# The first attention group in plain 128-key blocks, with the probabilities as matmul weights and copies on the chip for the second group

## The chip, the cores and the metric

The kernel runs on 1 core of one Trainium2 chip. Its time is the device time of one launch in microseconds (us), as the median of the runs that are fast. Engines are named as in the profile: PE is TensorE, PEld its weight loads, DVE is VectorE, ACT is ScalarE, POOL is GpSimd, SP is SyncE. A number like L728 is a line of the kernel that was profiled, so the same piece of code has another number in another version.

## The reference, cut to what matters

```python
# attention: batch 4, heads 8, sequence 768, head_dim 64; n_sink 4, window 64
# is_retrieval = [1, 0, 1, 0, 0, 0, 1, 0]
scores = (q @ k.T) / sqrt(64)
causal = rel >= 0                                  # rel = query position - key position
stream_keep = causal & (is_sink | (rel < window))  # heads 1, 3, 4, 5, 7
mask = causal for heads 0, 2, 6 else stream_keep
a = exp(scores masked - max); a = a / (a.sum(-1) + 1e-9)
x = (a @ v) reshaped to [3072, 512]
# mixture of 4 experts over all 3072 rows
p = domain_probs / (domain_probs.sum(-1) + 1e-9)
out = sum over e of p[:, e] * (relu(x @ w1[e]) @ w2[e])    # w1 512x1024, w2 1024x512
```

## The kernel before: the parts that the change touches

The 3072 rows are worked in eight groups of 384 queries (4 batches, two chunks each). A group is its attention, then four experts. PE runs group g's experts with the attention of group g+1 woven in between. Only the first group's attention has nothing to lie beside, so everything that it takes is in the time of the kernel. That stage, and the hand-over to group 1, is what the change rewrites.

In the kernel before, the first group uses the same forms as the others. Streaming heads take tiles of 96 keys with the four sink keys put in front of each; those sink rows are copied on DVE:

```python
def sink_row(b, h, c):                       # [cut: L261 is this copy]
    t = v_tile(b, c, h)[:, :, own(h)]
    nc.vector.tensor_copy(
        out=t[0:NS, TC * c : TC * (c + 1), :],
        in_=t[R0 : R0 + NS, 0:1, :].to_broadcast([NS, TC, D]),
    )
...
for h in range(H):                           # q and k of the first group: 16 loads
    nc.sync.dma_start(out=k32[:, :, h, :], in_=rows_of(k, 0, h, 0))
    nc.scalar.dma_start(out=q32[:, :, h, :], in_=rows_of(q, 0, h, 0))
nc.scalar.add_instruction(...)               # load of the table of functions, behind them
...
# values(h), cut: v is the weight, the probabilities move; 64 more columns of ones
# give the sum, and the quotient is exp(-ln(sum)) on ACT
nc.tensor.matmul(out=ps[:, q0 : q0 + nq], lhsT=v_tile(b, c, h)[:, t, :],
                 rhs=es[:, o : o + nq], ...)
nc.scalar.activation(out=rc[r, :], in_=ps[o, 0:CH], func=AF.Ln, bias=eps[o, :])
nc.scalar.activation(out=rc, in_=rc, func=AF.Exp, scale=-1.0)
nc.vector.tensor_tensor(out=xT[g][r, hp, :], in0=ps[r, 0:CH], in1=rc[r, :], op=ALU.mult)
...
def bank():                                  # scores, transposes and experts share these
    return pA.tile([P, 512], FP32, name="pA", bufs=4)
...
warm_up(ps_warm, 8, 512)
for _ in attention(0, 0):
    pass
zero(gp, kRr)                                # POOL memsets, behind POOL's weight loads
zero(gp, kSr)
mask_w()
# [cut] loop over groups: attention(g + 1) is woven into moe_group(g)
begin = {0: 0.2, 1: 1.0}.get(g, 0.0) * UNIT  # where the weaving begins
```

The softmax here doesn't subtract the row's maximum and nothing guards it: scores larger than these inputs give would overflow.

## Time and profile before

| what | value | read from |
|---|---|---|
| time | 414.77 us, 3 runs (413.07 to 414.81) | the runs |
| span of the profiled run | 413.1 us | head of the page |
| PE busy | 395.8 us (96%) | busy table of the page |
| granted PE clock | 1.00 in every stretch of the first 60 us | windows |
| first exponent on ACT | 9.09 us | timeline |
| first expert matmul, first relu | 24.30 us, 26.93 us | timeline |
| PE waits beside group 1's first transposes | 0.29 and 0.95 us | timeline |

The runs of this kernel fall on two values, about 413.07 and 414.8 us, so its median moves between these from one set of rounds to the next; a difference under 1.5 us says little unless the rounds are many. PE is busy from 24 us to the end. The stage up to the first relu is therefore the one place where time can be saved, and waits on PE beside group 1 are the one place where a change to this stage can add some. PSUM is the memory that PE's matmuls write to; a bank is a part of it. A warm-up is a matmul on a dummy tile, whose result nobody reads. Two timeline columns are read throughout: the start of a group of instructions (first number) and, in brackets at the end, how long its engine was idle just before and what ended that.

### The profile page before, as it was taken

Reading aid. Unit: us, or ns where it says so; the run is one execution under the profiler, and the core shown is the slowest. Engines: PE = TensorE matmul, PEld = TensorE weight load, DVE = VectorE, ACT = ScalarE, POOL = GpSimd, SP = SyncE. Lnnn points to the kernel's source line nnn. Section 1 sums busy time; section 2 is a strip of 40 time slices with the busy share of each in tenths; the row PEclk is TensorE's granted clock in tenths of the full one; section 3 lists DMA queues with packets and bytes.
Section 4 is the critical chain, followed back from the end, with each engine's and each line's share of the span. In section 5 each row is a group of like instructions: output and inputs, shape, how many; then the busy total and the mean of one; then the engine's idle time right before and its main releaser. Section 6 shows DMA issues by size and latency. Waiting matters only on the chain.

```text
span 413.1 us, 6801 instructions
## 1 busy us (share of the span) xinstructions
PE 395.8 (96%) x2670; PEld 222.4 (54%) x2670; DVE 155.8 (38%) x302; ACT 240.9 (58%) x509; POOL 141.7 (34%) x176
## 2 busy tenths in 40 slices
PE   6799999999999999999999999999999999999996
PEld 3565555555555555555555555555555555555552
DVE  7975553223433325233333333233343222432222
ACT  2676874336876547656665448566565477653331
POOL 8938618359359177002930085000000000000000
PEclk9999999999999999999999999999999999999999
DMA  9999999999989999058984999259002000020002
GB/s 173 142 195 204 209 208 133 136 210 124 174 64 181 217 75 101 27 107 147 111 53 96 182 72 77 17 108 166 2 2 76 5 2 0 2 76 2 1 2 76
DMA packets 159988, 40.83 MB, mean 99 GB/s; under 512 B 150364, under 2 KB 154836, under 8 KB 159956
## 3 DMA queue, kind: packets, MB, share of 16 engines
q0 software_dynamic: 102592, 20.98, 59.5%
q1 hardware_dynamic: 54164, 18.62, 21.7%
q10 hardware_dynamic: 3200, 0.79, 0.9%
q8 instruction: 21, 0.34, 0.3%
q14 instruction: 11, 0.09, 0.1%
HBM read 43.57 MB, written 6.29 MB: 121 GB/s over the span
## 4 chain that ended last, share of the span: by engine, by line
PE 86%; ACT 6%; DVE 4%; DMA 2%; issue 1%; ACTq 0%; DVEq 0%
PE pO L749 40%; PE pA L728 36%; PE pV L609 5%; PE pA L561 4%; ACT hs L741 2%; DMA q<-in_q_dram 2%; ACT rc L628 2%; DVE kS L490 1%; ACT rc L638 1%; DVE vS L261 1%; ACT es L579 1%; DVE kR L474 1%; DVE qT L465 0%; PE pO L355 0%; PE pV L355 0%
## 5 line engine op out<-in xcount | busy, mean ns | idle before, releaser
L728 PE MATMUL pA<-xT,w1sb 128*128 128x384 f16 x1024 | 187.4, 326 | 3.9 <-ACT hs L741 2.5
L749 PE MATMUL pO<-w2sb,hs 128*128 128x512 f16 x768 | 180.8, 379 | 0.0
L741 ACT ACTIVATE hs<-pA 128x384 f16<-128x384 f32 x256 | 122.1, 494 | 95.9 <-PE pA L728 89.1
L728 PEld LDWEIGHTS <-w1sb 128*128 128x128 f16 x1024 | 96.8, 98 | 65.5 <-issue 5.5
L749 PEld LDWEIGHTS <-hs 128*128 128x128 f16 x768 | 72.7, 98 | 74.3 <-ACT hs L741 0.6
L765 DVE SCALAR_TENSOR_TENSOR acc<-pO,p_sb,acc 128x512 f32<-128x512 f32 x72 | 53.9, 749 | 99.5 <-PE pO L749 98.9
L579 ACT ACTIVATE es<-pA 128x512 f16<-128x512 f32 (+3 forms) x122 | 61.0, 511 | 22.7 <-PE pA L561 20.9
L628 ACT ACTIVATE rc<-pV,eps 64x384 f32<-64x384 f32 x60 | 34.5, 575 | 33.0 <-PE pV L609 32.0
L204 POOL DMA_DIRECT2D kSr<-in_k_dram x30 | 30.1, 1006 | 36.5 <-issue 14.7
L250 POOL DMA_DIRECT2D vS<-in_v_dram x30 | 30.4, 1024 | 34.8 <-PE pV L609 34.0
L633 DVE TENSOR_TENSOR xT<-pV,rc 64x384 f16<-64x384 f32 x60 | 33.1, 552 | 4.2 <-PE pA L728 1.7
L583 DVE TENSOR_TENSOR es<-es,mW 128x384 f16<-128x384 f16 x30 | 10.8, 360 | 57.2 <-ACT es L579 57.2
L638 ACT ACTIVATE rc<-rc 64x384 f32<-64x384 f32 x58 | 30.2, 521 | 1.8
L761 DVE TENSOR_SCALAR acc<-pO,p_sb 128x512 f32<-128x512 f32 x24 | 18.0, 749 | 34.3 <-PE pO L749 33.0
L200 POOL DMA_DIRECT2D kRr<-in_k_dram x18 | 14.1, 783 | 47.2 <-DMA kR<-kRr 43.2
L583 DVE TENSOR_TENSOR es<-es,mC 128x256 f16<-128x256 f16 (+1 forms) x42 | 10.8, 257 | 45.4 <-ACT es L579 45.0
L561 PE MATMUL pA<-qT,kR 128*128 128x384 f16 (+2 forms) x120 | 25.0, 278 | 0.4
L609 PE MATMUL pV<-es,vR 128*128 128x384 f16 (+2 forms) x120 | 21.6, 278 | 0.0
L246 POOL DMA_DIRECT2D vR<-in_v_dram x24 | 19.2, 800 | 4.3 <-DMA w2sb<-in_moe_w_dram 4.2
L561 PEld LDWEIGHTS <-kS 128*128 128x128 f16 x255 | 13.9, 98 | 9.5 <-issue 2.9
L561 PE MATMUL pA<-qT,kS 128*128 128x55 f16 (+4 forms) x255 | 16.6, 195 | 2.2 <-ACT es L579 1.6
L609 PEld LDWEIGHTS <-vS 128*128 128x128 f16 x255 | 13.2, 98 | 9.1 <-DVE vS L261 3.0
(77 smaller groups left out, 161.3 us busy)
## 6 DMA issues: line engine op xcount, KB each, us to landing
out_dram<-acc SPq DMA_DIRECT2D x24, 256.0 KB
w1sb<-in_moe_w_dram POOLq DMA_DIRECT2D x4, 1024.0 KB, 14.5
w2sb<-in_moe_w_dram POOLq DMA_DIRECT2D x4, 1024.0 KB, 17.5
kSr<-in_k_dram POOLq DMA_DIRECT2D x30, 112.0 KB, 3.8
vS<-in_v_dram POOLq DMA_DIRECT2D x30, 112.0 KB, 3.8
q<-in_q_dram POOLq DMA_DIRECT2D x18, 128.0 KB, 4.4
vR<-in_v_dram POOLq DMA_DIRECT2D x24, 48.0 KB, 4.1
kRr<-in_k_dram POOLq DMA_DIRECT2D x18, 48.0 KB, 4.1
```

The lines of the kernel that those rows point to most:

```text
L204: gp.dma_start(out=kSr[:, :, SH.index(h), own(h)], in_=windows_of(k, b, h, c),)
L250: gp.dma_start(out=t[:, :, own(h)], in_=windows_of(v, b, h, c))
L561: nc.tensor.matmul(out=ps[:, o : o + nq], lhsT=key_tile(b, c, h, t), rhs=qTs[b, c][:, hp, q0 : q0 + nq], start=(n == 0 or not first), stop ...
L579: nc.scalar.activation(out=es[:, 0:cols], in_=ps[:, 0:cols], func=AF.Exp, scale=SC)
L609: nc.tensor.matmul(out=ps[:, q0 : q0 + nq], lhsT=v_tile(b, c, h)[:, t, :], rhs=es[:, o : o + nq], start=(n == 0), stop=(n == len(work) - 1 ...
L628: nc.scalar.activation(out=rc[r, :], in_=ps[o, 0:CH], func=AF.Ln, bias=eps[o, :])
L633: nc.vector.tensor_tensor(out=xT[g][r, hp, :], in0=ps[r, 0:CH], in1=rc[r, :], op=ALU.mult)
L638: nc.scalar.activation(out=rc[r, :], in_=rc[r, :], func=AF.Exp, scale=-1.0)
L728: nc.tensor.matmul(out=pss[ft][:, 0:CH], lhsT=w1sb[:, e * DMP + ct, ft * P : (ft + 1) * P], rhs=xT[g][:, ct, :], start=(ct == 0), stop=(ct ...
L741: nc.scalar.activation(out=hs[:, ft, :], in_=ps[:, 0:CH], func=AF.Relu)
L749: nc.tensor.matmul(out=ps_o, lhsT=hs[:, ft, j * P : (j + 1) * P], rhs=w2sb[:, e * FTP + ft, :], start=(ft == 0), stop=(ft == FTP - 1),)
L765: nc.vector.scalar_tensor_tensor(out=acc[nt], in0=ps_o, scalar=p_ap, in1=acc[nt], op0=ALU.mult, op1=ALU.add,)
```

## The change

The intent is a shorter first stage. Keys come in plain blocks of 128, with a band of biases for the streaming heads, so no sink rows are needed in that stage. In the value matmuls the probabilities are the weights, and v with one column of ones moves: 12 matmuls of 65 columns for a pair of heads. The quotient is then per row, done by DVE, and PE transposes the result. Half the heads of q and k, and all of v, come through GpSimd loads whose pieces are three rows long; PE puts v's rows in order again with a selection matrix. Since the next group expects keys and values in the old tiles, 37 small DVE copies make these afterwards.

```diff
-    for h in range(H):
-        nc.sync.dma_start(out=k32[:, :, h, :], in_=rows_of(k, 0, h, 0))
-        nc.scalar.dma_start(out=q32[:, :, h, :], in_=rows_of(q, 0, h, 0))
+    HF = H // 2
+    for h in range(HF):
+        nc.sync.dma_start(out=qk32[:, 1, :, h, :], in_=rows_of(k, 0, h, 0))
+        nc.scalar.dma_start(out=qk32[:, 0, :, h, :], in_=rows_of(q, 0, h, 0))
...
+    load_triples(v, v16, 0, 0)
+    band()
+    load_triples(k, qk16[:, 1, :, :, :], 0, 0, HF)
+    load_triples(q, qk16[:, 0, :, :, :], 0, 0, HF)
+    band_with_sinks()
...
+        def scores_own(h):                       # 64 rows, 64 rows, then biases: 128 rows
+            ps = bank()
+            score(ps, 0, h, 2, P, True)
+            score(ps, P, h, 0, CH, False)
+            if RETR[h]:
+                add(ps, 0, bC)
+            else:
+                add(ps, 0, bW[:, 0:P])
+                add(ps, P, bWs)
+            own_of[h] = exp(ps, 512)
...
+        def v_blocks():                          # 9 matmuls of 512 columns, 3 casts
+            for t in range(3):
+                ps = pO.tile([P, DM], FP32, name="pO", bufs=2)
+                for j in range(3):
+                    x = t * P - j + 2
+                    nc.tensor.matmul(out=ps, lhsT=pick[:, x : x + P], rhs=v16[:, :, j, :],
+                                     start=(j == 0), stop=(j == 2))
+                nc.vector.tensor_copy(out=v0[t][:, :, 0:D], in_=...)
...
+        WARM = [4, 4, 6, 8, 2, 2, 4, 4]          # warm-ups before values and quotients
+        transposes(0); scores_own(0); transposes(1); scores_own(1)
+        scores_shared(0, 2); scores_shared(1, 3)
+        transposes(2); v_blocks(); values(0); scores_own(2); scores_own(3)
+        transposes(3); values(1); to_xT(0, ...)
+        # [cut] the same for the other two pairs
...
+    def keep_for_next():
+        copy = nc.vector.tensor_copy
+        for h in range(H):                       # 4 copies a retrieval head, 5 a streaming one
+            ...
-    for _ in attention(0, 0):
-        pass
+    first_attention()
+    small_things()
+    keep_for_next()
```

(The calls that stand on one line here with semicolons stand on lines of their own in the kernel.)

## The prediction

> **What bounds the kernel now.** I read the busy table by stage first, then the chain of waits, then the timelines of the first 33 us. The view of windows (columns: stretch, its length, then busy us of PE, PEld, DVE, ACT and POOL with instruction counts, clock, DMA share, GB/s) gives, joined from two questions:
>
> ```profile
> 12.00:14.00 2.00, 1.31 (x9) 0.87 (x9) 1.94 (x6) 1.41 (x4) 2.00 (x3) 1.00 1.19 70
> 14.00:16.00 2.00, 1.47 (x16) 1.17 (x17) 1.93 (x7) 0.99 (x2) 2.00 (x4) 1.00 0.96 135
> 16.00:18.00 2.00, 0.87 (x7) 0.53 (x6) 2.00 (x1) 1.95 (x6) 2.00 (x3) 1.00 1.11 205
> ...
> 24.50:62.00 37.50, 34.64 (x267) 20.06 (x266) 22.46 (x43) 27.50 (x62) 18.09 (x25) 1.00 1.28 205
> 62.00:100.00 38.00, 37.73 (x215) 20.14 (x213) 9.54 (x16) 18.28 (x39) 26.26 (x29) 1.00 1.70 152
> ```
>
> From 62 us on PE has nothing left to gain; from 24.5 to 62 it idles 37.50 - 34.64 = 2.9 us. The change edits nothing after the first group but the work put in front of group 1. So it can pay only by letting the first expert matmuls start earlier, and cost only by making PE wait beside group 1. The timeline shows how the first stage runs and ends (start, us, engine, line, operation, count, idle before):
>
> ```profile
> 7.80 1.28 ACT L330 ACT_TABLE_LOAD   x1 [7.80 <-DMA q<-in_q_dram]
> 9.09 0.87 ACT L579 ACTIVATE es<-pA 128x512 f16<-128x512 f32 x2
> ...
> 12.83 1.63 DVE L261 COPY vS<-vS 4x256 f16<-4x256 f16 x1
> 15.73 2.72 DVE L261 COPY vS<-vS 4x256 f16<-4x256 f16 x1
> 21.30 0.22 DVE L261 COPY vS<-vS 4x256 f16<-4x256 f16 x1
> ...
> 24.30 3.09 PE L728 MATMUL pA<-xT,w1sb 128*128 128x384 f16 x16
> 25.96 0.56 DVE L633 TENSOR_TENSOR xT<-pO,rc 64x384 f16<-64x384 f32 x1 [0.60 <-ACT rc L638]
> 26.93 1.64 ACT L741 ACTIVATE hs<-pA 128x384 f16<-128x384 f32 x4 [1.01 <-PE pA L728]
> ```
>
> The scores' exponent starts only at 9.09, because ACT issues eight q loads (the later four wait for earlier ones) before its table load. Two tiny copies of sink values hold DVE 1.6 and 2.7 us and PE behind them. The first relu, the real end of the stage, is at 26.93. Then group 1's transposes need DVE at once:
>
> ```profile
> 27.94 0.79 DVE L474 CAST kR<-pA 64x384 f16<-64x384 f32 x1 [1.43 <-PE pA L457]
> 28.77 0.81 DVE L490 CAST kS<-pA 64x384 f16<-64x384 f32 x1
> 29.63 0.36 PE L457 MATMUL pA<-ident,q 128*64 128x128 f16 x6 [0.29 <-DVE kS L490]
> 31.91 0.82 PE L728 MATMUL pA<-xT,w1sb 128*128 128x384 f16 x4 [0.95 <-DVE kS L490]
> ```
>
> Here the reader sees that PE's expert matmuls and the transposes share four PSUM banks, so that PE already stops (0.29, 0.95 us) until DVE has emptied one.
>
> **What the Trainium skill says.** (1) "SBUF — State Buffer", section "Who interferes with whom": a DVE copy in a two-port mode and a GpSimd instruction take one shared port pair as an exclusive lock. The trace agrees: the same 4x256 copy takes 0.22 us at 21.30 and 2.72 us at 15.73, while POOL runs memsets back to back. (2) "VectorE: DVE Perf Modes", section "The TRN2 errata": 58 + FD/4 cycles at 0.96 GHz for a 16-bit SBUF copy, that is 0.08 us at 64 elements; for 128x256 it gives 0.127, and the trace has 0.14 from the mask copy at 21.55 to the next at 21.69. (3) Same page, section "Two Vector instructions with no wait between them": an instruction that starts in another 32-partition quadrant is held until the one before has finished. The trace fits: after the 0.54 us cast to partitions 0 to 63 at 5.60, the one to 64 to 127 starts at 6.17; the next, in the same quadrant, follows after 0.48. (4) "TensorE: Matmul & The Clock Gate", Part 1: about 3.4 us of idle PE halve its clock. PE's longest wait in this trace is 1.7 us (at 7.28), so no run shows it yet.
>
> **The change part by part.**
>
> *Loads and start.* HWDGE loads fall from 16 to 8; ACT's fourth issue ends at 2.97 in the trace, so the table load ends near 4.3, not 9.09. PE's eight cold warm-up matmuls still run until 4.65, so the first transposes stay at 4.65. The first exponent: K transposes end 4.99, K cast ready 5.76; q copy on ACT ready 6.03; score and mask 0.33 plus 0.21 latency (traced between a matmul's last column and its reader): 6.6 instead of 9.1, 2.5 us early.
>
> *Until the values.* Then transposes(1), its ACT copy, and own scores of head 1 at 8.04; two shared tiles to 9.14. Transposes(2) needs the half loaded by GpSimd: POOL order from traced durations (masks 1.5, issues 0.8 to 0.9 each, selects 0.56) puts the issue of k at 5.3 and q at 6.1; with 3.6 us landing I estimate 9.8 for q. The row-ordering of v is new PE work: 9 matmuls of 512 columns at 0.216 = 1.94 us, the third block held for one of two pO banks. Its last cast, 0.70 us, is ready at 13.37. So the first values finish at 13.95; before, heads 0 and 1 had theirs at 15.0. The 2.5 us have shrunk to about one.
>
> *PE in order from 13.6.* Issue slots: 128 columns 0.056, 384 columns 0.1625; a value matmul with 65 columns 0.06 (traced 0.28 for five of 64 columns). Own scores 6 x 0.33 to 0.43 = 2.4; last transposes 0.76; shared 0.66; three pairs of values, twelve matmuls each, 2.0 (0.18 of it overlapped); the warm-ups between, 4+2+2+6+4 of 256 columns at 0.109 = 2.0; xT transposes 0.5. That brings PE to 21.8 with almost no wait. The end is serial: eight warm-ups 0.87, values(3) 0.72 to 23.38, latency and small DVE ops to 24.08, quotient to 24.64, transpose to 24.85, cast of xT to 25.6. Expert matmuls run 24.85 to 26.80 and their first relu starts near 27.1. Before: 26.93. **The stage gains nothing by this sum, +0.2 us**: the v blocks, transposes of the quotient and longer PE order use up what the table load, the sinks, the logarithm and the 13 ACT operations of the old quotient gave back.
>
> *Group 1's copies.* On DVE, in order, after the last xT cast (issued to 25.55): nine small operations 1.55 us (before, inside the stage), then 12 copies for three retrieval heads and 25 for five streaming heads. From (2): 3 x 0.16 + 9 x 0.08 + 20 x 0.08 + 5 x 0.18 = 3.7 us; (3) adds three holds of 0.09 in each of five heads, 1.3. So DVE is free at 25.55 + 1.55 + 5.0 = 32.1. POOL by then issues loads (v blocks until about 29, weights after), no memsets, so I add no lock. The first kR cast, possible at about 28.0, starts at 32.1: **+4.0 us**, with PE stopped at the fourth transpose for want of a bank and nothing behind it free to run. If the clock falls in a wait of that length, another 1.7 us at most; I give it 0.3.
>
> *The rest.* Weights: before, w1 landed at 20.5 and was used at 24.3; second set landed 36.6, used 41.4. Larger pieces land earlier, so no PE wait on loads. Fewer sink copies in group 1's own transposes: about -0.5 us of DVE, in time that the copies of before fill; I put -0.2. Sum: 414.8 + 0.2 + 4.0 + 0.3 - 0.2 = 419.1.
>
> **The rivals.** (a) *The stage shortens by 2 to 4 us and the copies cost little*: 411 to 413. For it: warm-ups of 4, 6 and 8 matmuls look chosen where PE waits anyway, so that my PE sum may carry 2 us that are not real; the copies may be waited for by nobody if banks come free in another order. Against it: the chain above is PE-bound from 13.6, and the begin of group 1's steps was left as it was. (b) *DVE lock*: POOL's issues of whole-tensor loads block two-port copies as at 12.83 (1.63 us during the issues of k and q). Three or four such hits in 37 copies, and a cold clock: 422 to 425. Before, 48 KB v loads beside a copy did not block it (0.2 us at 19.65), which speaks against. (c) *Late halves of q and k*: landing at 11.5 instead of 9.8 adds about 1.7 to the stage: 420 to 421.
>
> **Range and chances.** My sum says 419.1. I shade it to 418.0, since an in-order sum of a stage usually errs by carrying warm-ups as costs. Range 411.5 (rival a) to 422.5 (low end of b). Over 2% faster means under 406.5, a stage of 16 us, which the PE work alone forbids: 0.04. Over 2% slower means above 423.1, rival (b) with a cold clock: 0.10. Within: 0.86.
>
> **What would show it.** In the changed profile: table load ended by 4.5 and first exponent at 6.5 to 7.5; q's second half landed by 10; last v cast at 13 to 14; first expert matmul at 24 to 26 and first relu at 26 to 28; 37 short DVE copies over 4 to 8 us; an idle of 3 to 5 us on PE, put down to DVE's kR or kS cast, with the two q and k transposes around it; nothing changed from 70 us on except the shift. Wrong if the first expert matmul comes before 22 (then the PE sum is wrong), if no PE wait on DVE above 1.5 us stands beside group 1 (then the bank argument is wrong), or if single copies of over 1 us appear (then the lock was under-rated).

## The result, and the profile after

| | before | after |
|---|---|---|
| time, median of 4 | 413.92 us (413.06 to 414.81) | 430.45 us (428.99 to 430.67) |
| span of the profiled run | 413.1 us | 427.3 us |
| first relu | 26.93 us | 31.37 us |
| ratio after / before | | 1.0392, 95% interval 1.0353 to 1.043 |

A ratio, here and below, is the mean time of one kernel's fast runs over that of the other's of the same rounds, so it is not quite the ratio of the medians quoted. Executions over 1.5% slower than the fastest of the same kernel are left out of the means. The change makes the kernel 3.9% slower; the prediction was 418.0 with a range up to 422.5.

The page of the kernel after: the busy table's row of PE, the granted clock in 40 slices (tenths of full speed), and the costliest group (busy us, mean ns, then the idle time before it and what ended most of it).

```profile
PE 405.0 (95%) x2724; PEld 225.3 (53%) x2724; DVE 156.1 (37%) x322; ACT 236.6 (55%) x492; POOL 143.4 (34%) x186
...
PEclk9897899999999999999999999999999999999999
...
L899 PE MATMUL pA<-xT,w1sb 128*128 128x384 f16 x1024 | 188.3, 327 | 12.1 <-DVE kS L518 9.0
```

PE is busy 9 us longer than before, the clock is below full in slices 2, 4 and 5 (of 10.7 us each, so between 10.7 and 53.4), and the expert matmuls waited 9.0 us for one DVE cast. The timeline of the kernel after shows where.

```profile
7.21 0.60 ACT L728 ACTIVATE es<-pA 128x512 f16<-128x512 f32 x1 [0.68 <-PE pA L721]
...
11.65 0.36 PE L707 MATMUL pA<-ident,qk 128*64 128x128 f16 x6 [0.78 <-DMA qk<-in_q_dram]
11.94 3.43 PE L772 MATMUL pO<-q,pick 128*128 128x512 f16 x9
...
29.06 2.76 PE L899 MATMUL pA<-xT,w1sb 128*128 128x384 f16 x16
31.37 1.64 ACT L912 ACTIVATE hs<-pA 128x384 f16<-128x384 f32 x4 [4.51 <-PE pA L899]
34.07 0.36 PE L491 MATMUL pA<-ident,q 128*64 128x128 f16 x6 [0.29 <-ACT hs L912]
43.47 1.46 PE L899 MATMUL pA<-xT,w1sb 128*128 128x384 f16 x4 [9.04 <-DVE kS L518]
```

The first exponent does come early, at 7.21 instead of 9.09. By the first relu that is lost: 31.37 against 26.93, or 4.4 us late. Then PE runs the first four groups of transposes of group 1 (two for k and two for q, the last at 34.07) and stops for 9.04 us. Where the kernel before waited 0.95 us for the cast of keys, the kernel after waits for it behind the copies. The windows of the same kernel (columns as in the prediction) show what else follows.

```profile
34.40:37.00 2.60, 0.02 (x1) 0.00 (x0) 2.60 (x2) 0.00 (x0) 2.57 (x3) 0.90 1.24 207
37.00:40.00 3.00, 0.00 (x0) 0.00 (x0) 2.89 (x13) 0.00 (x0) 2.74 (x8) 0.50 1.21 210
40.00:43.40 3.40, 0.00 (x0) 0.00 (x0) 3.35 (x12) 0.00 (x0) 3.40 (x4) 0.50 1.12 210
43.40:46.40 3.00, 2.78 (x9) 1.25 (x10) 2.92 (x6) 1.08 (x2) 0.99 (x2) 0.50 1.23 206
```

PE does nothing from 34.4 to 43.4, its clock falls to one half within that time, and stays there for the 3 us of work after it. DVE is busy all along. What DVE and POOL do in it is in their timelines:

```profile
33.13 0.89 POOL L278 DMA_DIRECT2D w2sb<-in_moe_w_dram  x1 [1.85 <-DMA w1sb<-in_moe_w_dram]
33.18 3.82 DVE L873 COPY kS<-kS 64x20 f16<-64x20 f16 x1
33.25 3.77 DVE L879 COPY vS<-v 64x64 f16<-64x64 f16 x1
34.01 0.61 POOL L298 MEMSET kRr<- 128x576 f32 x1
34.52 2.00 POOL L298 MEMSET kSr<- 128x2240 f32 x1
36.43 0.54 POOL L395 MEMSET mW<- 128x495 f16 x1
37.05 0.72 POOL L396 TENSOR_SCALAR_AFFINE_SELECT mW<-mW 128x495 f16<-128x495 f16 x1
...
40.63 1.01 POOL L212 DMA_DIRECT2D kSr<-in_k_dram  x1
...
41.03 0.60 DVE L880 COPY vS<-v 32x64 f16<-32x64 f16 x1
```

Two copies of 64x20 and 64x64 elements end at 37.00 and 37.02. They stood from 33.2 on, while POOL ran a load issue and three memsets without a gap; POOL's first gap is 36.97 to 37.05, and there both copies end. The copies before that had gone at 14 in 1.94 us (31.32 to 33.26), 0.14 us each. After it there are four shorter holds, about 1.6 us together: at 37.22, 37.87 and 39.2 beside POOL's selects and small memsets, and at 41.03, where a copy that takes 0.17 us elsewhere took 0.60 while POOL ran nothing but a load issue. In the kernel before, POOL comes to the same memsets later:

```profile
37.78 0.60 POOL L303 MEMSET kRr<- 128x576 f32 x1
```

**Where the 14.2 us of span lie.** Take one point of the program that both profiles have: group 1's first scores before the first expert's second layer. It is at 33.44 us before and 47.60 after, so the whole difference is made up to there. Of the 14.2 us, 4.4 come up to the first relu. From that relu to the point the kernel before takes 6.5 us and the kernel after 16.2, 9.7 us more: PE's idle time grows from 1.24 to 9.48 us (8.2), and the half clock after it takes about 1.5.

### The profile page after: what moved, and what is told of

Read it like the earlier page. It is cut to its first block, busy times and chain, and to the rows that moved or that the text cites. A ratio compares the mean times of both kernels' runs of the same rounds, so it can differ in the third digit from the quotient of the medians.

```text
span 427.3 us, 6900 instructions
## 1 busy us (share of the span) xinstructions
PE 405.0 (95%) x2724; PEld 225.3 (53%) x2724; DVE 156.1 (37%) x322; ACT 236.6 (55%) x492; POOL 143.4 (34%) x186
## 4 chain that ended last, share of the span: by engine, by line
PE 84%; ACT 7%; DVE 4%; issue 2%; DMA 2%; POOL 1%; POOLq 0%
PE pO L920 38%; PE pA L899 33%; PE pV L610 4%; PE pA L576 4%; ACT hs L912 3%; ACT rc L628 2%; DMA qk<-in_q_dram 2%; ACT es L585 1%; DVE kS L873 1%; ACT rc L637 1%; PE pO L772 1%; PE pV L358 1%; PE pA L734 1%; PE pV L796 1%; PE pA L721 1%
## 5 line engine op out<-in xcount | busy, mean ns | idle before, releaser
L585 ACT ACTIVATE es<-pA 128x384 f16<-128x384 f32 (+2 forms) x106 | 54.7, 522 | 22.0 <-PE pA L576 21.7
L628 ACT ACTIVATE rc<-pV,eps 64x384 f32<-64x384 f32 x56 | 32.2, 575 | 32.8 <-PE pV L610 31.9
L633 DVE TENSOR_TENSOR xT<-pV,rc 64x384 f16<-64x384 f32 x56 | 30.9, 552 | 4.0 <-PE pA L899 1.7
L637 ACT ACTIVATE rc<-rc 64x384 f32<-64x384 f32 x56 | 29.2, 521 | 1.8
L576 PE MATMUL pA<-qT,kR 128*128 128x384 f16 (+2 forms) x111 | 23.3, 281 | 0.4
L610 PE MATMUL pV<-es,vR 128*128 128x384 f16 (+2 forms) x111 | 20.1, 278 | 0.0
L254 POOL DMA_DIRECT2D vR<-in_v_dram x21 | 16.8, 798 | 0.6 <-DMA w2sb<-in_moe_w_dram 0.6
L576 PEld LDWEIGHTS <-kR 128*128 128x128 f16 x111 | 10.9, 99 | 10.2 <-issue 1.7
L576 PEld LDWEIGHTS <-kS 128*128 128x128 f16 x235 | 12.2, 98 | 7.3 <-issue 0.7
L186 POOL DMA_DIRECT2D q<-in_q_dram x18 | 16.0, 906 | 0.0
## 6 DMA issues: line engine op xcount, KB each, us to landing
w1sb<-in_moe_w_dram POOLq DMA_DIRECT2D x3, 1024.0 KB, 16.2
```

The costliest lines, as they stand in the source:

```text
L576: nc.tensor.matmul(out=ps[:, o : o + nq], lhsT=key_tile(b, c, h, t), rhs=qTs[b, c][:, hp, q0 : q0 + nq], start=True, stop=True,)
L585: nc.scalar.activation(out=es[:, 0:cols], in_=ps[:, 0:cols], func=AF.Exp, scale=SC)
L637: nc.scalar.activation(out=rc[r, :], in_=rc[r, :], func=AF.Exp, scale=-1.0)
```

## The experiments

The theory after reading the two traces was this. (1) The copies cost about 10 us: they are a block on DVE in front of group 1's casts, the block is doubled by the port that DVE's fast copies share with POOL, and the clock falls in the wait. (2) The stage costs 4 to 5 us: from late halves of q and k, from alternation between 64-row and 128-row matmuls, from a half clock at the v matmuls, and from warm-ups on PE's path. Rivals stand with each run. All results were correct unless it is said otherwise.

### A. The copies

**e1_two_input: the copies in a form with two inputs.**

```diff
-        copy = nc.vector.tensor_copy
+        def copy(out, in_):
+            nc.vector.tensor_tensor(out=out, in0=in_, in1=in_, op=ALU.max)
```

> The 37 copies for group 1 as two-input maximum of a thing with itself, same data, same order, same DVE queue. Theory (the shared port lock): of the 10.5 us that the copies took, 5.8 are lock, in four or five single copies that lie beside POOL memsets; a two-input form needs no shared write port, so no memset holds it. Then the copies take 5 to 6.5 us, no single one over 0.7 us, the PE wait on DVE falls from 9.0 to about 4 us, the half clock after it shortens or goes, and the time falls by 5 to 7 us to 424 to 425.5. Rival (the copies are slow of themselves or wait for POOL's fills of kR and vS): all as before, 430.4 within 1 us.

Measured: 427.04 us (426.52 to 427.34), ratio to before 1.0315 (1.0281 to 1.0349), so 3.4 us under the kernel after. The timeline of e1 (one line is a group of two or three copies; the two POOL and PE lines are what stands beside and after):

```profile
35.00 0.71 DVE L859 TENSOR_TENSOR vS<-v 64x64 f16<-64x64 f16 x3
35.55 2.00 POOL L298 MEMSET kSr<- 128x2240 f32 x1
...
38.81 1.08 DVE L859 TENSOR_TENSOR vS<-v 64x64 f16<-64x64 f16 x3
...
41.47 1.46 PE L901 MATMUL pA<-xT,w1sb 128*128 128x384 f16 x4 [5.70 <-DVE kS L518]
```

The same memset of 2.00 us now holds up nothing: three copies beside it take 0.71 us, as they do with no memset near. Only beside the selects at 38 to 40 us, which read SBUF, are they slower (1.08). The copies take 7.2 us (32.64 to 39.82) instead of 10.5, though the two-input form is slower by itself, and PE waits 5.70 instead of 9.04. So the lock is shown, with 3.3 us of wait. The time fell less than expected because the stage of the profiled run was slower (its first expert matmul is about 1.3 us later) and the block itself, and the half clock after it, are still there.

**e2_begin_later: group 1 begins a whole expert later.**

```diff
-        begin = {0: 0.2, 1: 1.0}.get(g, 0.0) * UNIT
+        begin = {0: 1.2, 1: 1.0}.get(g, 0.0) * UNIT
```

> Group 1's steps begin after 1.2 instead of 0.2 units of expert work (12.5 instead of 2.1 us). Theory (the copies cost only because the transposes hold PSUM banks until DVE comes to them): PE's 9.0 us wait vanishes, no half clock at 36 to 46 us; time falls by 9 to 10.5 us to 420 to 421.5, though the copies take as long as they did. Rival (DVE's work itself is what ends last, or expert matmuls need the banks whatever the order): no more than 3 us.

Measured: 430.22 us (429.54 to 431.34), ratio 1.0396. Nothing gained. The timeline of e2:

```profile
33.67 3.83 DVE L879 COPY vS<-v 64x64 f16<-64x64 f16 x1
...
41.97 3.57 PE L920 MATMUL pO<-w2sb,hs 128*128 128x512 f16 x8 [4.62 <-DVE acc L932]
```

With no transpose in the four shared banks, PE runs on into the second layer of the first expert. There it waits 4.62 us for DVE all the same (and the eight matmuls after the wait take 3.57 us, at half clock), this time for the result `acc` to be taken out of PSUM, queued behind the same copies. Group 1's attention, now squeezed, adds waits of 0.53 to 0.60 us by 54 us. My narrower reading (the bank that the transposes fill is what stops PE) falls; the rival holds: DVE's queue is blocked as a whole, and everything in front of which it stands has to wait.

**e5_gaps: the copies spread into gaps of the stage.** Heads 1, 3, 4 and 5 in two-input form on DVE, the retrieval heads on ACT, one streaming head left at the end, and the nine small operations early.

```diff
         transposes(1)
+        small_things()
         scores_own(1)
...
         to_xT(0, nc.vector.tensor_copy)
+        keep([1, 3])
...
         values(2)
+        keep([4, 5])
...
         to_xT(2, nc.scalar.copy)
+        keep(RH, nc.scalar.copy)
...
     first_attention()
-    small_things()
-    keep_for_next()
+    keep([7])
```

> The same 37 copies, spread over idle time of the first stage: sink heads on DVE as two-input copies in its gaps, retrieval heads on ACT while it waits for the first relu; the nine small operations after the second transposes. Theory (copies cost only as a block on DVE between the stage and group 1, by PE's 9.0 us wait and by the 1.5 us of half clock that follows): no PE wait on DVE over 1.5 us beside group 1, no half clock after 30 us, time 419 to 421.5. Rival (later begin of group 1's steps showed that DVE work must be paid somewhere): the stage grows by the copies instead, first relu 2 us or more later than 31.4, time 423 or more.

Measured: 423.30 us (421.51 to 424.19), ratio 1.0216. The PE waits beside group 1 are those of the kernel before again (0.96 and 0.22 us), with a whole clock there. But the first relu comes at 34.98: the small operations, put early, waited 3.12 us on DVE for the load of the expert probabilities, and one of them stood 2.05 us in the lock. That was a mistake of this experiment, not a finding on the change. PE also ran at half speed until about 20 us in this profile, with the clock column at 1.00, so the late relu is not the mistake's alone.

**e9_gaps_fixed: the same with that mended** (small operations after the third values, heads 4, 5 and 7 at the end).

```diff
-        small_things()
         scores_own(1)
...
         values(2)
-        keep([4, 5])
+        small_things()
...
-    keep([7])
+    keep([4, 5, 7])
```

> The gaps version mended: there the nine small operations stood where DVE waited 3.1 us for the domain probabilities to land and 2.1 us in one operation beside POOL, which put the first relu at 34.98. Here they stand after the third quotient; sink heads 1 and 3 after the first xT cast, 4, 5 and 7 after the last, retrieval heads on ACT. Theory (copies cost only as a block in front of group 1): first relu at 30.5 to 32, no PE wait on DVE over 1.5 us beside group 1, time 418.5 to 420.5. Rival (the copies' time comes back in the stage): first relu above 33, time 422 or more.

Measured: 420.10 us (418.82 to 420.60), ratio 1.0126 (1.0098 to 1.0153). That is 10.3 us under the kernel after, by moving the copies and the nine small operations and changing the copies' form (those of the retrieval heads now on ACT), with no other work removed. The longest PE wait on DVE beside group 1 is 1.0 us. First relu and one window of e9:

```profile
13.00:16.00 3.00, 3.00 (x11) 1.04 (x8) 0.79 (x2) 0.80 (x1) 2.94 (x8) 0.52 1.25 206
...
32.58 1.64 ACT L918 ACTIVATE hs<-pA 128x384 f16<-128x384 f32 x4 [1.84 <-PE pA L905]
```

Its first relu is even later than that of the kernel after (32.58 against 31.37), so all of the gain, and 1.2 us more, is after the relu. Theory (1) holds with its size: the block of copies, its lock and the clock cost about 10 of the 15.6 us. What is left, 420.1 against 414.9, is the stage. The window shows a half clock in it.

**e8_before_sinks: the lock in the kernel before.** Its sink copies in two-input form.

```diff
-        nc.vector.tensor_copy(
-            out=t[0:NS, TC * c : TC * (c + 1), :],
-            in_=t[R0 : R0 + NS, 0:1, :].to_broadcast([NS, TC, D]),
+        x = t[R0 : R0 + NS, 0:1, :].to_broadcast([NS, TC, D])
+        nc.vector.tensor_tensor(
+            out=t[0:NS, TC * c : TC * (c + 1), :], in0=x, in1=x, op=ALU.max
         )
```

> The kernel before with one edit: its five sink copies, 4x256, as a two-input maximum. Theory (port lock): none takes over 0.45 us (they took 1.63 and 2.72 at worst); PE's 3.4 us of waits for them at 14.5 and 18.5 shrink, first expert matmul 1.5 to 3 us earlier than 24.3, time 411 to 412.5. Rival (PE's order or the ACT chain binds the stage there): copies short but time within 1 us of 413.9.

Measured: 413.43 us (412.49 to 414.55), before in the same rounds 414.79, ratio 0.9982 (0.9947 to 1.0017): unclear. The copies that took 1.63 and 2.72 us take 0.28 and 0.27, and in the profile the first relu comes at 24.71 instead of 26.93. So the lock is the same in the kernel before. The profiled spans differ by 2.2 us too (413.1 and 410.9), but that of before is a run of its slower value and that of e8 one of its faster; value against value (412.5 and 414.4 against 413.07 and 414.8) e8 gains about 0.5 us. The median gains 1.4 us with an interval that holds 1. So whether the earlier relu shortens the kernel isn't shown.

### B. The stage

**e4_k128: scores over 128 rows, a wrong form.** Both heads of a pair are summed, so that no matmul has 64 rows. The number of matmuls and columns is the same. (Attention over such small scores is close to a mean, and the check of the result passed all the same.)

```diff
-            hp, u = divmod(h, 2)
-            r = slice(u * D, (u + 1) * D)
+            hp = h // 2
+            r = slice(0, P)
```

> Wrong result on purpose: the first group's scores contract over all 128 partitions (both heads of a pair) instead of the 64 of one, same column counts, same count of matmuls. Theory (a switch between a 64-row and a 128-row matmul costs about 0.1 us, as own scores take 0.54 to 0.64 us in the trace where their columns make 0.33 to 0.43): own scores take 0.33 to 0.43 us, the first expert matmul comes 1.5 to 2.2 us earlier, time 428.3 to 429. Rival (the matmul durations come from something else, such as waits for ACT): no change within 0.4 us.

Measured: 428.41 us (426.70 to 429.41), ratio 1.0346, 2.0 us under the kernel after. Scores and biases of a shared tile in the timeline of the kernel after, then of e4; the first column is the start.

```profile
19.85 0.25 PE L734 MATMUL pA<-qT,kS 64*128 64x192 f16 x1
20.04 0.26 PE L721 MATMUL pA<-bW,ident 128*128 128x192 f16 x1
```

```profile
19.85 0.25 PE L734 MATMUL pA<-qT,kS 128*128 128x192 f16 x1
19.93 0.25 PE L721 MATMUL pA<-bW,ident 128*128 128x192 f16 x1
```

The bias follows its score after 0.19 us in one and 0.08 in the other: a change between 64 and 128 rows costs about 0.11 us. The last transpose of the quotient starts at 27.35 instead of 28.88, 1.5 us earlier. The prediction had issue slots for these matmuls and no term for the change.

**e14_fill_pairs** tests the same with a right result further down.

**e3_fill: warm-ups before the two transposes that wait for late halves.**

```diff
+                if hp == 2:
+                    warm_up(ps_fill, 6, 256)
                 ps = bank()
```

> Six idle matmuls of 256 columns ahead of each of the two transposes that wait for the second half of k and q. Theory (PE's clock halves at about 12 us because PE has had too little to do from 8.5 to 11.9): the clock stays whole, the nine 512-column v matmuls take 1.95 instead of 3.23 us, the warm-ups behind them 0.45 instead of 0.85; first expert matmul 1.3 to 1.7 us earlier than 29.06, time 428.7 to 429.2. Rival (the slow v matmuls are no matter of the clock, or it falls in its own rhythm): v matmuls stay above 3 us, time same or up to 0.5 us longer.

Measured: 429.08 us (428.25 to 430.69), ratio 1.0371. 1.4 us under the kernel after, within the scatter of both. In its profile the clock is whole from 10 to 18 us and the nine v matmuls take 2.41 us instead of 3.43, but the last quotient's transpose starts at 28.82 against 28.88: what the clock gave, the fills and the casts of v took back. e2, whose code is that of the kernel after up to 30 us, kept a whole clock there without any fill. So the half clock in the stage comes in some runs and not in others, and the time of e3 alone settles nothing. e13 takes it up again.

**e6_gaps_loads and e7_gaps_loads_cold**, on top of e5: loads of the halves of k and q issued first, own scores of heads 2 and 3 moved ahead of the waiting transposes; then fewer warm-ups as well.

```diff
+    load_triples(k, qk16[:, 1, :, :, :], 0, 0, HF)     # e6
+    load_triples(q, qk16[:, 0, :, :, :], 0, 0, HF)
     mask_c(bC, 0.0, -60000.0)
     load_triples(v, v16, 0, 0)
...
-        WARM = [4, 4, 6, 8, 2, 2, 4, 4]                # e7
+        WARM = [0, 0, 0, 4, 0, 0, 0, 4]
```

> On top of the gaps version: second halves of k and q issued first on POOL, ahead of the causal mask and of v; own scores of heads 2 and 3 placed ahead of the transposes that wait for those halves. Theory (1.3 us of PE waits at 10 to 12 us, and the clock that may fall there, are the late second halves: they landed at 10.5 and 11.65 where I had estimated 9.8): PE waits on these loads under 0.4 us in sum, first relu 1 to 2 us earlier than in the gaps version, time 1 to 2 us below it. Rival (v is what the values wait for, so nothing is gained by k and q): the v matmuls wait for v instead, within 0.5 us of the gaps version.

> On top of the version with earlier loads: 26 of the 34 warm-up matmuls taken out. Theory (PE bounds the stage from 16 us on, so warm-ups lie on the path): first relu up to 2.4 us earlier, time 1 to 2.4 us lower than with them. Rival (they only fill waits or keep the clock whole): no gain, or half clock in the stage and a longer time.

Measured: e6 421.80 us (ratio 1.0182), 1.5 under e5, first relu 33.23 instead of 34.98. e7 420.38 us (ratio 1.0149), 1.4 under e6. Both in the direction of the theory; but e5 carried the mistake told above, and the three profiles differ in speed as well (e6 is at a clock of 0.50 from 10 to 16 us, e7 from 10 to about 19), so neither gain is shown to be its edit's.

**e10_fixed_loads_cold: e6's and e7's edits on e9.** Its edit is the sum of the two above.

> The mended gaps version, with k and q halves first, own scores of heads 2 and 3 ahead of the transposes that wait for them, and 26 warm-ups fewer. From the earlier steps (1.5 us for the loads, 1.4 for the warm-ups): first relu 28 to 29.5, time 415.5 to 417.5, still above the kernel before: the v matmuls, the row-count switches and the longer PE order stay. Rival (what is left of the change is no slower than before): 414 or less.

Measured: 420.96 us (420.33 to 424.20), ratio 1.0174. A miss: no better than e9. Its windows say why. From 8 to 10 us PE is busy 1.10 of 2 us, and from 10 to 18 the clock is at 0.50; matmuls take double. With fewer warm-ups and other loads first, PE has more holes early on, and loses in clock what it saves.

**e11_rows_v: e10 with v loaded by rows**, so that neither v matmuls nor their casts are needed.

```diff
-    load_triples(v, v16, 0, 0)
+    for j in range(3):
+        gp.dma_start(
+            out=v0[j][:, :, 0:D],
+            in_=v[0, :, j * P : (j + 1) * P, :].rearrange("h p d -> p h d"),
+        )
...
-        v_blocks()
```

> On top of that: v of the first group loaded by rows in three transfers with 256-byte source pieces straight into its blocks, so no matmuls that put rows in order, no casts of v on DVE, no selection matrix. Theory (the v blocks, 1.95 us of PE at full clock and 3.2 at half, are on the path): first relu 1.5 to 3 us earlier, time 413 to 415.5. Rival (longer pieces pay for it: v lands later by rows and the values wait for it): PE waits over 1.5 us on v, no gain.

Measured: 421.24 us (420.57 to 421.58), ratio 1.0156. The v work is gone, and the clock stood at 0.50 from 10 to 28 us in the profile, so that this run settles nothing about the v blocks.

**e13_fixed_fill: e9 with e3's fills, and the other warm-ups left out except before the last pair.**

```diff
+                if hp == 2:
+                    warm_up(ps_fill, 6, 256)
...
-        WARM = [4, 4, 6, 8, 2, 2, 4, 4]
+        WARM = [0, 0, 0, 8, 0, 0, 0, 4]
```

> e9 (420.10 us) with six warm-up matmuls before each of the two transposes that wait for the late halves (as in e3), and the 22 warm-ups of the values and the transposed quotient left out except before the last group (12 stay). Theory (half clock at the v matmuls, and warm-ups on a path where PE is busy without a break from 16 to 29 us): the nine v matmuls take 2.0 to 2.5 us instead of 3.5, 22 warm-ups of 0.109 us or 2.4 us leave the path, first relu at 29.5 to 31 instead of 32.58, time 416.5 to 418.5. Rival (the late quotient, ACT and the DVE copies bind the later part, so PE merely waits where warm-ups stood; or the clock halves again with fewer of them, as in e10): 420 to 421.

Measured: 417.14 us (416.98 to 421.27, four of five within 0.5), ratio 1.0056 (1.0039 to 1.0073), 3.0 under e9. The time is as the theory had it. But two things changed at once, fills put in and 22 warm-ups taken out, and the only profile is of the run of 421.27, so what each is worth, and that the clock was whole in the fast runs' stage, is not shown. In it PE was slow from its first matmuls into the v matmuls although the clock column says 1.00; six warm-ups in the timeline of e13, beside the same six in that of e16 further down, show it:

```profile
11.95 1.49 PE L358 MATMUL pV<-warm 128*128 128x256 f16 x6
```

**e14_fill_pairs: e13 with the scores of two heads before the biases of both**, half as many changes of row count, the same matmuls, a right result.

```diff
+            pss = [bank() for h in heads]
+            for h, ps in zip(heads, pss):
+                score(ps, 0, h, 2, P, True)
+                score(ps, P, h, 0, CH, False)
+            for h, ps in zip(heads, pss):
+                ...                                    # biases and exponent, as before
...
-        scores_own(2)
-        scores_own(3)
+        scores_own(2, 3)
```

> e13 with the score matmuls (64 rows) of two heads before the bias matmuls (128 rows) of both, so that the number of changes between 64 and 128 rows is halved; right result, same matmuls. Theory (each change costs PE about 0.1 us, in e4 1.5 us in all): PE's busy time before the first expert matmul falls by 0.6 to 0.9 us, time 0.5 to 1 us under e13. Rival (e4's gain came from something else, such as two halves of rows that could not run beside each other): no more than 0.2 us from e13, or slower because the exponent starts later.

Measured: 417.73 us, with two runs at 416.5 and two at 418.9 (ratio 1.0069). The profiled run is one of the slow pair, with PE at half speed early on as in e13's profile. Two values against e13's 417.1: unclear. The mechanism is e4's; that this order gains time is not shown.

**e15_fill_rows_v: e13 with v by rows**, the three loads spread between the others so that k and q are issued no later, and two heads' scores ahead of the first values.

```diff
-    load_triples(v, v16, 0, 0)
+    v_rows(0)                       # v_rows(j): the load of e11 for one j
     band()
...
+    v_rows(1)
     band_with_sinks()
+    v_rows(2)
...
         transposes(2)
-        v_blocks()
-        values(0)
         scores_own(2)
         scores_own(3)
         transposes(3)
+        values(0)
         values(1)
```

> e13 with v loaded by rows in three loads (no v matmuls, no v casts), own scores of heads 2 and 3 and the fourth transposes ahead of the first values. Theory (the v blocks lie on PE's path with 1.94 us at full clock, as the prediction's sum had it): first relu 1.5 to 2.5 us earlier than in e13, time 1.5 to 2.5 us under it, if the clock stays whole and the halves of k and q land no later. Rival (the loads by rows, or the late halves, hold the first values as long as the v blocks did): within 0.5 us of e13 with PE waits on DMA before the first values.

Measured: two fast runs of 413.91 and 414.05 us, ratio 0.9979 (0.9959 to 0.9999), and two runs of 423.25 us that are slow (their granted clock reads as whole as that of the fast ones; I don't know what they are). By the fast ones 3.2 us under e13. That is the worth of the edit as a whole: it takes out the v blocks and their casts, and it also moves two heads' scores and the fourth transposes ahead of the first values; the shares aren't shown.

**e16_fill_rows_v_pairs: e14 and e15 together.** No new edit.

> e14 and e15 together, right result. Theory (clock, warm-ups, row changes and v blocks are the whole of what is left of the stage's excess after e9): about 414, level with the kernel before (414.87), and the terms add: its difference from e13 is the sum of those of e14 and e15 within 0.7 us. Rival: the terms don't add and it stays at 417 or above.

Measured: 413.90 us (413.89 to 415.14), ratio 0.9984 (0.9969 to 0.9999), level with the kernel before (414.84 in these rounds). The timeline of e16:

```profile
9.50 0.82 PE L356 MATMUL pV<-warm 128*128 128x256 f16 x6
...
23.54 2.76 PE L898 MATMUL pA<-xT,w1sb 128*128 128x384 f16 x16
25.86 1.64 ACT L911 ACTIVATE hs<-pA 128x384 f16<-128x384 f32 x4 [1.83 <-PE pA L898]
```

First relu 25.86, a microsecond before that of the kernel before. The pairs add nothing to e15 (0.1 us): the time that PE saves turns into a wait of 1.08 us for the quotient of the third pair. So the loss of the change is undone step by step: 10.3 us by the copies (e9), 3.0 by fills and warm-ups (e13), 3.2 by v and the new order (e15), 16.5 in all, against 15.6 to win back in these rounds' medians (430.45 to 414.84). These are medians of several rounds on three chips; before's own median lay between 413.9 and 414.9 there, so I take the sum as good to about a microsecond.

**e17_swap: is there more?** The small operations into DVE's gap, the copies of heads 1 and 3 behind the third quotient, and the eight warm-ups before the last values left out.

```diff
-        WARM = [0, 0, 0, 8, 0, 0, 0, 4]
+        WARM = [0, 0, 0, 0, 0, 0, 0, 4]
...
         to_xT(0, nc.vector.tensor_copy)
-        keep([1, 3])
+        small_things()
...
         values(2)
-        small_things()
+        keep([1, 3])
```

> e16 (413.90 us) with two things changed on the last part of the stage, to see whether a version can beat the kernel before: the nine small DVE operations stand in the gap of 1.1 us where DVE waited for the zeros of GpSimd at 16 to 17 us, the copies of heads 1 and 3 after the quotient of the third pair, and the eight warm-ups before the last values are left out. Theory (the quotient of the third pair was held about a microsecond behind those copies, and the warm-ups of 0.87 us lie on the path): first relu 1 to 2 us earlier than e16's 25.86, time 412 to 413, just under the kernel before (414.8, with some runs at 413.1). Rival (the last values wait for the exponent on ACT and the DVE copies only change places): within 0.4 us of e16.

Measured: 414.48 us (413.39 to 414.99), before in the same five rounds 413.08 (413.05 to 414.81), ratio 1.0016 (0.9993 to 1.0039). A miss. The timeline of e17 has the first expert matmuls earlier and slower, and the windows say why (first fence: timeline of e17; second: windows of e17; third: the same window of e16; fourth: timeline of e17).

```profile
22.98 4.29 PE L898 MATMUL pA<-xT,w1sb 128*128 128x384 f16 x16
```

```profile
20.00:22.00 2.00, 1.01 (x10) 0.62 (x10) 1.91 (x9) 1.98 (x9) 1.81 (x5) 1.00 1.42 201
...
24.00:26.00 2.00, 2.00 (x8) 0.99 (x7) 1.92 (x11) 0.00 (x0) 2.00 (x4) 0.50 1.31 203
```

```profile
20.00:22.00 2.00, 1.51 (x22) 1.37 (x22) 1.90 (x9) 1.42 (x5) 1.81 (x5) 1.00 1.43 201
```

From 20 to 22 us PE is busy 1.01 us in e17 and 1.51 in e16. The clock falls to one half at about 22.7 us, just as the expert matmuls begin, and these take 4.29 us instead of 2.76; the first relu is at 26.81, 0.95 later than e16's. But three things changed. The copies of heads 1 and 3 now stand in DVE's queue before the last quotient, which starts at 21.66, and PE waits 1.63 us for it where e16's waits 0.64; the clock falls at the end of that wait:

```profile
22.68 0.50 PE L818 MATMUL pO<-ident,x 128*128 128x128 f16 x3 [1.63 <-DVE x L807]
```

Whether the missing warm-ups, the wait made by the moved copies, or both let the clock fall is not shown; a run with only the warm-ups left out would tell.

**e12_before_table: the other gain of the change, alone, in the kernel before.** e8's sinks, and the load of the table of functions between the sixth and seventh load of q; five rounds.

```diff
         nc.scalar.dma_start(out=q32[:, :, h, :], in_=rows_of(q, 0, h, 0))
+        if h == 5:
+            nc.scalar.add_instruction(...)              # the table load, from below the loop
```

> The kernel before with the two-input sink copies and with ACT's table load between its sixth and seventh q issue, where ACT waits for earlier loads anyway. Theory (the first exponent waits for the table load until 9.09): first exponent at 7.8 to 8.2, first relu 2.2 to 3.3 us earlier than 26.93, time 410.5 to 412.5. Rival (ACT, busy without a break from 13 to 24 us, is not helped by an early start since the loads of later heads bind): as with the sink copies alone, 412.5 to 414.

Measured: 414.26 us (413.62 to 414.97), ratio 0.9989 (0.9967 to 1.001). No gain. The table load ends earlier, but the last two loads of q are now issued behind it, at 8.11 us, and the first exponent starts at 9.11 as before. Those issues end at 9.03; the profile puts the exponent's wait down to PE's scores, which begin at 8.58 instead of 7.96 and end just before it too. Either alone would have held it, so the table load was not the last thing that it waited for, and which of the two binds isn't shown. This profile also has a half clock from about 9 to 12 us, which those of before and e8 have not (first relu 26.45, against e8's 24.71), so the time does not decide between theory and rival.

No version here beats the kernel before beyond its own scatter; e15 and e16 are level with it.

## Why the prediction was wrong, by its own steps

**Right.** The first exponent came early (predicted 6.6, measured 7.21). The stage did not gain from it. PE stopped behind the fourth group of transposes of group 1, with the two q and k transposes around it, put down to DVE's cast. The clock fell in that wait. No wait for weights appeared. And all change lies before 48 us; from there on the two profiles only stand apart by the shift.

**Wrong, the main step: "POOL by then issues loads (v blocks until about 29, weights after), no memsets, so I add no lock".** Both sides of that step moved. The prediction had the copies at 27.1 to 32.1 us; the stage was late and they ran from 31.3. And it took POOL's order from the kernel before, where the memsets of kRr and kSr run from 37.78 us; with the loads of the kernel after POOL reached them at 34.01, 3.8 us earlier. So copies and memsets met, which in the predicted schedule they would not have done (its copies end at 32.1, and the memsets begin at 34.01); that the memsets were so near, a margin of a few microseconds behind copies that PE waits for, was not weighed. But the step's ground fails in itself too: load issues can hold a copy. The long hold begins within one (33.13 to 34.02), the copy at 41.03 stood 0.60 us with nothing else on POOL, and in e2 copies of 0.64 and 0.42 us stand at 30.46 and 31.36 beside issues. Not every copy beside an issue is held (those from 40.66 to 41.02 are not), and what the issues alone would have cost in the predicted schedule is not shown. The term "37 copies, 5.0 us" was right for copies that nothing holds: 14 of them went at 0.14 us each, 5.1 us for 37. It measured 10.5; two copies alone stood 3.8 us. The +4.0 us on PE became +8.2 (e1 shows the lock, e9 the size of the whole). The prediction's rival (b) named the lock, as three or four short hits; it came as one long one of 3.7 us and four short ones of about 1.6 us together.

**Wrong, a size: the half clock, 0.3 us.** With the wait at 9.04 us instead of 4, the clock was at one half when PE went on, and that cost about 1.5 us.

**Wrong, a size: "The stage gains nothing by this sum, +0.2 us."** The first relu came 4.4 us late. The terms that were missing or too small: (a) changes between 64 and 128 rows, for which the sum of issue slots had nothing, 1.5 us in the stage (e4); (b) the second half of q, estimated to land at 9.8 and used at 11.65 us, with 0.55 and 0.78 us of PE wait; (c) the half clock at the v matmuls in this profile, 3.43 us instead of 2.41 in e3's with a whole clock, of which part reaches the end. The sum knew only that a long wait can halve the clock; here it fell in some runs, and in others not, where no single wait was over 0.8 us. (a) to (c) are measured in separate runs, and overlap, so they are not a sum to the tenth. The v blocks were in the sum, with 1.94 us on PE; taking them and their casts out, with a new order of scores and transposes, gave 3.2 (e15). That much the intended gain of longer load pieces had to earn and did not.

**Wrong, the shading.** The sum of 419.1 was lowered to 418.0, since warm-ups might not be real costs. Of the two directions it was the wrong one, and the chances followed the sum: "slower by over 2%" was given 0.10.

**Open.** Why the early part of some runs is at half speed with the clock column at 1.00 (e5, e13, e14): every profile here starts so (512 columns of the first warm-ups take 0.43 us, later ones 0.216), but in the kernel after this ends by about 7 us, in e14 near 14, e13 near 18, e5 near 20; what lets the clock fall in short waits; what the two runs of 423 us of e15 are; how far the order of e14 gains when nothing else waits.

## What to carry to other kernels

Work that is moved off a stage's path onto an engine's queue is paid when that queue is next needed: look for the next instruction on that engine that someone waits for, and spread the moved work into gaps before it (e9: 10.3 us for the same copies in another place). When many small fast DVE copies will run, look up what POOL runs at just that time in the new schedule, not in the old one, load issues included, or use a two-input form, which no memset held here (e1). And before calling warm-up matmuls a cost, look whether PE waits where they stand, and compare the clock and the time with and without them, one edit at a time; these runs give no threshold for it.

## What the Trainium skill lacked or had wrong

- "SBUF — State Buffer", section "Who interferes with whom", says that who issues first has the shared pair "for the whole instruction". Here POOL kept it over four instructions back to back, a load issue and three memsets: a DVE copy of 64x64 stood 3.77 us, until POOL's first gap of 0.08 us. That two-input DVE instructions are held only by POOL instructions that read SBUF agrees: 0.71 us for three beside a memset, 1.08 beside a select (e1).
- "TensorE: Matmul & The Clock Gate", section "Part 1: The HAM clock gate (the "warmup" mystery)", ties the half clock to an idle window of about 3.4 us. The 9.04 us wait agrees in part: the clock fell about 2.1 us into it (PE idle from 34.43, clock 1.00 until 36.4, 0.50 from 36.6). It also fell with no single wait over 1.7 us (e17, at 22.7 us; the kernel after, at 12.6, with PE busy 0.70 us of the two before 12). No busy share that suffices is given there, and none comes out of these runs: e2, whose code is the same up to there, kept its clock with 0.52 us of those two, and the kernel before with 0.87 of two (16 to 18).
- The same section warns that traces of clock events can be unreliable; the case here is a clock that reads 1.00 while matmuls run at half speed: six warm-ups of 256 columns took 1.49 us in e13's profile and 0.82 in e16's, both at 1.00. Every profile here starts with matmuls at that half speed under a column of 1.00.
- "TensorEngine Tiling (Array Packing)", section "Key Properties", says that a change of tiling mode drains PE, and gives no time. Here is one for alternating between 64-row and 128-row matmuls: a following matmul of 192 columns starts 0.19 us after the one before instead of 0.08 (e4), 1.5 us over this stage.
